# FNet mixing with a hard-swish MLP: gathers for the special piece of x, the first two weight pieces joined behind x, the last piece folded and multiplied in two parts

## The chip, the cores and the metric

The kernel runs on one core of a Trainium2 chip. The metric is the device time of one execution in microseconds (us), as the median of several runs. The core has a matrix engine (TensorE, "PE", with its weight loads "PEld"), a vector engine (VectorE, "DVE"), a scalar engine (ScalarE, "ACT"), GpSimd ("POOL") and SyncE ("SP"), which here only issues DMAs. DMAs are issued by SP, ACT and POOL; 16 DMA engines carry them all.

## The reference

The input x is (8, 3008, 256). A 2D Fourier transform is taken over the last two axes and its real part kept; an MLP with hard-swish follows.

```python
X = np.fft.fft(x, axis=1)
X = np.fft.fft(X, axis=2)
x = X.real.astype(np.float32).reshape(B * S, D)     # 24064 tokens of 256
h = x @ w_in                                        # w_in 256 x 2048
g = h * np.clip(h + 3.0, 0.0, 6.0) / 6.0
out = g @ w_out                                     # w_out 2048 x 256
```

## The kernel before

**Factoring.** 3008 is 47 x 64, so a position is a row n1 (47 of them) and a column n2 (64). Stage 1 transforms over n1, stage 2 over n2; the transform over the 256 features is folded into w_in (`fold_w_in`, L788: a product with the table C gives W1, and its last row, sent by a DMA of one column at a time, gives WN). Before stage 1 x is folded: each element is added to its partner at the mirrored position, so that only 32 of the 64 columns remain.

**Pieces of x.** A batch of x is cut into pieces of four columns. The partners of a piece lie at mirrored rows and come by an indirect DMA on POOL, a gather by a list of row numbers IX (`gather`, L172). For the first two batches one piece holds four columns m of the first half on partitions 0 to 46 and four of the second half on partitions 64 to 110. The pieces are taken in the order `ORDER` = 3, 0, 1, 2. Piece 3 is the special one: its last column, on the upper partitions, is column 0, which does not follow the others. For the first batch, `load_half` (L188) loads piece 3 by three direct DMAs on POOL's queue (two blocks of rows and the slot of column 0) and the other pieces by gathers; partners always come by gathers. For the second batch all direct rows go out on SP's queue, those of piece 3 on POOL's.

**Start.** The whole opening is written out by hand, in this order. PE runs products with zeros (`keep_awake`) so that its clock stays up. SP loads FI (which holds IX), C and the stage-1 table F. POOL issues the loads of the first two weight pieces (`load_w`), then x of the first batch, then weight pieces 2 and 3. The weights arrive as 64-bit floats (w_in and w_out are float64) and are turned into 32-bit floats: ACT takes the exponent's bytes (`exponent_a`), PE expands them (`exponent_b`), ACT makes them a power of two (`exponent_c`), DVE takes the mantissa (`mantissa`) and multiplies the two (`join`); `tail` is exponent_c and join. Pieces 0 and 1 are joined and folded (`fold_w_in`) before x's folds in DVE's and PE's queues. Then, for each piece of x, DVE folds (`fold_half`, two parts) and PE does stage 1 (`stage1_early`, L304). Pieces 3 and 1 are "full": a y with sums and differences is made. Pieces 0 and 2 leave that to PE, which multiplies four column ranges instead. The results z are copied from PSUM by ACT (for the last piece one half by DVE) and written to DRAM (zd); after T, the stage-2 table, has been loaded, `load_g_half` reads the rows of the first group back as g. Stage 2 (L434), the copies q and qn, and the first chunk's products follow. POOL's next loads wait for g (`see`, L863).

**Main loop.** A chunk is 256 positions. For each of 8 steps fc, PE multiplies q with W1 (`mlp1_products`: u, v, PSUM tiles from three buffers that stage 1 and the exponents use too), DVE and ACT apply hard-swish (`activate`: s from qn, WN and u; then a), and PE multiplies a with G, the mixed w_out. In the first chunk this is the plain product (`mlp2_first`, L597), while the other weight pieces are still being converted; after it seven products replace eight (`mlp2`, L617), for which POOL adds parts of a to c (`combine`, L587) and mixes the blocks of w_out (`mix_w_out`, L777). A table in `beside` says at which step the rest is put: loads and folds of the second batch (folds on POOL), its stage 1 (`stage1_quarters`) and stage 2. All engines run their queues in the written order.

Of the kernel before, what the change touches and what calls it, by code (L numbers as in the profile page):

```python
# [7 lines left out]
F32 = mybir.dt.float32  # L8
# [5 lines left out]
AL = mybir.AluOpType  # L14
# [44 lines left out]
def kernel(  # L59
# [77 lines left out]

    ORDER = [NM - 1] + list(range(NM - 1))
    FULL = (ORDER[0], ORDER[2])

    def x_tile(pool=xpool, tag="x"):
        return pool.tile([P, XC, D], F32, tag=tag, name="xt")
# [42 lines left out]
    def take_half(hb, m, pool=xpool, tag="x"):  # L185
        hb.x[m], hb.xr[m] = x_tile(pool, tag), x_tile(pool, tag)

    def load_half(hb, m, queue):  # L188
        if hb.b == 0 and m < NM - 1:
            gather(hb.x[m], NP * NXC + m, P, D)  # L190
        for h in range(2 if hb.b or m == NM - 1 else 0):
            c = m + h * NM
            nr = N1 + 1 if h else PB
            n = XC if c < NXC - 1 else XC - 1
            rows, o = x_pn[hb.b * N1:hb.b * N1 + nr], hb.x[m][h * PB:h * PB + nr]
            queue.dma_start(out=o[:, 0:n, :], in_=rows[:, c * XC + 1:c * XC + 1 + n, :])
            if n < XC:
                queue.dma_start(out=o[:, n:XC, :], in_=rows[:, 0:1, :])
        gather(hb.xr[m], hb.b * NM + m, PX if hb.b else P)

    def fold_half(hb, m, part, eng):
        xt, xr = hb.x[m][0:PX - 1], hb.xr[m][0:PX - 1]
# [101 lines left out]
    def stage1_early(hb, m):  # L304
        cosine, sine = slice(0, P + 1), slice(P + 1, D)
        last = m == NM - 1
        y = hb.y.pop(m) if m in FULL else hb.x[m]
        pt = [ps_h.tile([P, 2, 1], F32, tag="uv", name="pt") for h in range(2)]
        ps = [bank([P, 2, D], "ps1") for h in range(2)]
        quarters = [(i, h, 1 if last and h and i else 2) for i in range(2) for h in range(2)]  # L310
        for i, h, n in quarters:
            o = pt[h][i * PB:(i + 1) * PB]
            nc.tensor.matmul(o[:, 0:n], table(5, h), y[rows(h), 2 * i:2 * i + n, P:P + 1], start=True, stop=True,
                             skip_group_check=True)
            for k in range(2 if n < 2 else 0):
                nc.tensor.matmul(o[:, 1], table(k + 1, h), y[rows(h), XC - 1 + k, P:P + 1], start=(k == 0),
                                 stop=(k == 1), skip_group_check=True)
        if m in FULL:
            for i, h, n in quarters:
                o = ps[h][i * PB:(i + 1) * PB]  # L320
                nc.tensor.matmul(o[:, 0:n], table(0, h), y[rows(h), 2 * i:2 * i + n], start=True, stop=(n == 2),
                                 skip_group_check=True)
                for k, (j, cs) in enumerate([(XC - 1, cosine), (XC, cosine), (XC - 1, sine), (XC, sine)] if n < 2 else ()):
                    nc.tensor.matmul(o[:, 1, cs], table(k + 1, h), y[rows(h), j, cs], start=False, stop=(k % 2 == 1),
                                     skip_group_check=True)
        else:
            back = slice(D - 1, P, -1)
            for k, (t, to, fr) in enumerate([(0, cosine, cosine), (0, sine, slice(1, P)),
                                             (0, slice(1, P), back), (6, sine, back)]):
                for i, h, n in quarters:  # L330
                    nc.tensor.matmul(ps[h][i * PB:(i + 1) * PB, :, to], table(t, h), y[rows(h), 2 * i:2 * i + 2, fr],
                                     start=(k == 0), stop=(k > 1), skip_group_check=True)
# [416 lines left out]
        nc.scalar.activation(exs[j].bitcast(I32), exs[j], AF.Identity, scale=2.0 ** 23)  # L749

    def mantissa(j):
        st = raw.pop(j)
# [105 lines left out]
    def tail(j):  # L858
        exponent_c(j)
        join(j)  # L860
# [10 lines left out]
                            channel_multiplier=1)  # L871
    nc.scalar.mul(E[:, 1], E[:, 0], -1.0)
    for k, m in enumerate(ORDER):
        load_half(hb, m, nc.gpsimd)
    for j in range(2, 4):
        load_w(j)
    for j in range(2):
        exponent_a(j)
        mantissa(j)
        exponent_b(j)  # L880
        keep_awake(1)
    exponent_c(0)
    exponent_c(1)
    clear_table(1)
    for j in range(2):
        join(j)
        fold_w_in(j)
    load_t(0)
    keep_awake(1)
    for k, m in enumerate(ORDER):  # L890
        for part in range(2):
# [7 lines left out]
    for j in range(4, 10):  # L899
        load_w(j)  # L900
    take_half(halves[1], ORDER[0], cpool, "c")
    load_half(halves[1], ORDER[0], nc.gpsimd)
# [12 lines left out]
    starting[0] = False  # L915
    spare = [ps_a.tile([P, 2, WB // 2], F32, tag="acc", name="spare") for h in range(2)]

# [4 lines left out]
    def beside(p):  # L922
# [7 lines left out]
        if p == 0:  # L930
            for gr in range(1, NG):
                put(gr + 1, load_t, gr)
            put(1, load_g_half, halves[0], 1)
            put(5, spread_half, halves[0], 1)
            put(NF - 1, close_w)
            for i, t in enumerate((3, 5, 7, 8)):
                put(t, mix_w_out, i)
            for gr in range(2, NSG):
                put(8 * gr - 10, load_g_half, halves[0], gr)
                put(8 * gr - 5, stage2_half, halves[0], gr)  # L940
                put(8 * gr - 4, spread_half, halves[0], gr)

            hb = halves[1]
            for k, m in enumerate(ORDER):
                if k > 0:
                    put((5, 8, 11)[k - 1], take_half, hb, m)
                    put((5, 8, 11)[k - 1], load_half, hb, m, nc.sync)
                for part in range(2):
                    put((4, 6, 11, 14)[k] + part, fold_half, hb, m, part, nc.gpsimd)
                put((8, 10, 15, 18)[k], stage1_quarters, hb, m, at=behind)  # L950
            for gr in range(NSG):
                put(8 * gr + 23, load_g_half, hb, gr)
                put(8 * gr + 27 - (gr == 0), stage2_half, hb, gr)
                put(8 * gr + 28 - (gr == 0), spread_half, hb, gr)
# [222 lines left out]
```

## Time and profile before

| | us |
|---|---|
| median of 3 runs | 1941.01 (1939.63 to 1941.74) |
| profiled execution | 1940.75 |
| its span in the trace | 1939.0 |
| PE busy | 1920.7 (99%) |
| DVE busy | 1426.0 (74%) |
| POOL busy | 1440.7 (74%) |
| ACT busy | 681.5 (35%) |
| mean granted PE clock | 0.998 |

Times in the trace count from the span's start. A group line names the source line, engine, operation and tiles, then busy time and the idle time before it with what ended it. The chain of waits follows the work that ended last back from the end; each piece has its start and length. A matmul in 32-bit floats shows as two passes. The main events of the start in the trace:

| event | us |
|---|---|
| DVE's first fold of x (L210) | 12.07 |
| PE's first stage-1 product (L313) | 15.91 |
| PE's last stage-1 pass ends | 23.40 |
| SP issues the read of g | 27.61 |
| PE's first stage-2 product (L434) | 30.43 |
| PE's first product with G (L597) | 38.37 |

### The profile page before, as it was taken

The numbers are of one execution on the slowest core, as the hardware profiler recorded it, in microseconds if no ns is written. First come the engines' busy times: TensorE is split into PE (matmuls) and PEld (weight loads), VectorE is DVE, ScalarE is ACT, GpSimd is POOL, SyncE is SP. The second block draws the span as 40 slices with busy tenths as digits, with TensorE's granted clock in tenths as the row PEclk, the third lists the DMA queues.
The fourth block names the chain that finished last, engine by engine and source line by source line (L and its number), as shares of the span: only waits on it lengthen the run. The fifth ranks groups of instructions, "written<-read, shape, count | busy, mean of one in ns | idle before, by whom it ended". The sixth has DMA issues, their size and how long they took to land.

```text
span 1939.0 us, 28126 instructions
## 1 busy us (share of the span) xinstructions
PE 1920.7 (99%) x9322; PEld 1652.9 (85%) x9322; DVE 1426.0 (74%) x2756; ACT 681.5 (35%) x1165; POOL 1440.7 (74%) x1647
## 2 busy tenths in 40 slices
PE   9999999999999999999999999999999999999997
PEld 5578888888988888888898888888899888888887
DVE  6867776767777777777787777777778777777777
ACT  6533333333333333333333333333333333333332
POOL 4397888886678877787678877878666667666664
PEclk9999999999999999999999999999999999999999
DMA  8522222311112222121111221122110101101000
GB/s 256 143 69 53 52 71 71 80 44 34 36 34 55 67 60 55 44 52 33 34 36 48 53 55 44 51 52 50 35 28 20 28 17 28 33 12 28 20 19 20
DMA packets 154472, 98.08 MB, mean 51 GB/s; under 512 B 121987, under 2 KB 136078, under 8 KB 154326
## 3 DMA queue, kind: packets, MB, share of 16 engines
q1 hardware_dynamic: 142898, 59.25, 12.6%
q0 software_dynamic: 10720, 36.81, 6.8%
q8 instruction: 73, 1.20, 0.3%
q14 instruction: 73, 0.60, 0.1%
q10 hardware_dynamic: 708, 0.23, 0.1%
HBM read 58.92 MB, written 37.32 MB: 50 GB/s over the span
## 4 chain that ended last, share of the span: by engine, by line
PE 93%; DVE 2%; POOL 1%; DMA 1%; ACT 1%; issue 1%; SPq 0%; ACTq 0%; DVEq 0%; POOLq 0%
PE acc L617 56%; PE v L524 16%; PE u L524 16%; PE ps L473 2%; PE ps L274 1%; PE acc L597 1%; POOL c L587 1%; DVE a L573 1%; DVE s L533 0%; PE ps L434 0%; ACT t L570 0%; PE spare L798 0%; DVE o L678 0%; DMA st<-in_moe_w_in_dram 0%; DMA WN<-W 0%
## 5 line engine op out<-in xcount | busy, mean ns | idle before, releaser
L587 POOL TENSOR_TENSOR c<-a 128x512 f32<-128x512 f32 (+1 forms) x375 | 469.3, 1251 | 352.4 <-PE acc L617 286.7
L617 PE MATMUL acc<-c,G 128*128 128x256 f32 (+1 forms) x3008 | 697.6, 375 | 1.2 <-POOL c L587 1.1
L570 ACT ACTIVATE t<-u,half 128x512 f32<-128x512 f32 (+1 forms) x384 | 260.7, 679 | 1145.0 <-DVE u L543 1065.5
L617 PEld LDWEIGHTS acc<-c,G 128*128 128x128 f32 x3008 | 565.0, 190 | 73.4 <-POOL c L587 2.4
L533 DVE SCALAR_TENSOR_TENSOR s<-qn,WN,u 128x256 f32<-128x256 f32 (+1 forms) x768 | 330.4, 471 | 345.0 <-PE u L524 337.8
L617 PE MATMUL acc<-a,G 128*128 128x256 f32 (+1 forms) x2256 | 541.6, 375 | 0.0
L617 PEld LDWEIGHTS acc<-a,G 128*128 128x128 f32 x2256 | 421.0, 189 | 73.6 <-issue 20.1
L524 PE MATMUL v<-q,W 127*128 127x256 f32 (+1 forms) x1536 | 389.6, 375 | 3.1 <-DVE a L573 3.1
L524 PE MATMUL u<-q,W 128*128 128x256 f32 (+1 forms) x1536 | 388.0, 375 | 0.2 <-ACT q L437 0.2
L573 DVE SCALAR_TENSOR_TENSOR a<-t,u 128x512 f32<-128x512 f32 (+2 forms) x448 | 263.9, 601 | 101.5 <-ACT t L570 98.3
L524 PEld LDWEIGHTS v<-q,W 127*128 127x128 f32 x1536 | 288.0, 190 | 44.0 <-DVE a L573 3.4
L524 PEld LDWEIGHTS u<-q,W 128*128 128x128 f32 x1536 | 285.8, 190 | 36.9 <-issue 1.9
L587 POOL TENSOR_TENSOR c<-a,c 128x256 f32<-128x256 f32 (+1 forms) x375 | 269.0, 717 | 29.4
L587 POOL TENSOR_TENSOR c<-c,a 128x256 f32<-128x256 f32 (+1 forms) x375 | 269.0, 717 | 29.4
L543 DVE TENSOR_TENSOR u<-s,v 128x512 f32<-128x512 f32 x352 | 245.1, 696 | 37.7 <-DVE s L533 1.4
L573 DVE SCALAR_TENSOR_TENSOR a<-t,v 128x512 f32<-128x512 f32 (+1 forms) x480 | 263.5, 565 | 1.1 <-ACT t L570 0.6
L570 ACT ACTIVATE t<-v,half 128x512 f32<-128x512 f32 (+1 forms) x384 | 260.8, 679 | 1.6 <-issue 1.0
L545 DVE TENSOR_TENSOR v<-v,s 128x512 f32<-128x512 f32 x352 | 243.9, 693 | 0.0
L587 POOL TENSOR_TENSOR r<-w,e 128x256 f32<-128x256 f32 (+1 forms) x92 | 88.8, 987 | 3.6
L627 ACT ACTIVATE e<-acc 128x512 f32<-128x512 f32 (+2 forms) x184 | 83.4, 544 | 0.0
L678 DVE STREAM_TRANSPOSE o<-r 128x256 f32<-128x256 f32 (+1 forms) x192 | 72.5, 415 | 0.2
L587 POOL TENSOR_TENSOR w<-w,e 128x512 f32<-128x512 f32 (+1 forms) x46 | 57.6, 1252 | 3.6
(128 smaller groups left out, 776.8 us busy)
## 6 DMA issues: line engine op xcount, KB each, us to landing
out_dram<-o SPq DMA_DIRECT2D x747, 32.0 KB
g<-zd SPq DMA_DIRECT2D x42, 256.0 KB
zd<-z SPq DMA_DIRECT2D x48, 192.0 KB
xt<-in_x_dram POOLq DMA_DIRECT2D x23, 256.0 KB
st<-in_moe_w_in_dram POOLq DMA_DIRECT2D x8, 512.0 KB
st<-in_moe_w_out_dram POOLq DMA_DIRECT2D x8, 512.0 KB
qn<-qd SPq DMA_DIRECT2D x16, 256.0 KB
xt<-in_x_dram POOLq DMA_DIRECT2D x17, 192.0 KB
```

What stands on the lines that cost most here:

```text
L274: nc.tensor.matmul(ps[b][h * PB:(h + 1) * PB, 0:n], F[rows(b), 0:PB], y[rows(b), 2 * h:2 * h + n], start=True, stop=not last, skip_group_c ...
L473: nc.tensor.matmul(ps[:, blk, u * P:n].rearrange("p (b k) -> p b k", b=2), g[:, kk, blk * (P + 1):blk * (P + 1) + P], T[:, :, gr, blk, kk, ...
L524: nc.tensor.matmul(ps[:, i, 0:nq], W1[r, blk, f * P:(f + 1) * P], q[r, blk, of:of + nq], start=True, stop=True)
L533: nc.vector.scalar_tensor_tensor(s[:, i, 0:nq], qn[:, of:of + nq], WN[:, f:f + 1], u[:, i, 0:nq], op0=AL.mult, op1=AL.add)
L543: nc.vector.tensor_tensor(u[:], s[:], v[:], op=AL.add)
L545: nc.vector.tensor_tensor(v[:], v[:], s[:], op=AL.subtract)
L570: nc.scalar.activation(t, h, AF.Relu, bias=half[:], scale=scale)
L573: nc.vector.scalar_tensor_tensor(dst, t, 1.0, h, op0=AL.min, op1=AL.mult)
L587: (eng or nc.gpsimd).tensor_tensor(out, in0, in1, op=AL.add)
L617: nc.tensor.matmul(ch.acc[i // 2][:, i % 2, 0:ch.n], G[:, i, fc, :], mv, start=(fc == 0 and i % 2 == 0), stop=(fc == NF - 1), skip_group_c ...
L627: nc.scalar.mul(ch.e[:, k:i + 1, 0:ch.n], ch.acc[i // 2][:, 0:i + 1 - k, 0:ch.n], 1.0 / WS)
L678: nc.vector.transpose(o[:, 0:n // DH, h], ch.r[:, m, h, 0:n].rearrange("p (j i) -> p j i", i=DH))
```

## The change

Five edits go together.

1. The special piece of x is gathered like the others, for both batches, and the second batch's other pieces too; all are issued by POOL. The gathered piece has a wrong last column on the upper partitions. For the first batch SP loads the right one early, into a tile of its own, and ACT copies it in; for the second SP loads it into place at step 1 (`load_zero`). The kernel's tables already hold the row numbers.
2. The load of T moves from behind the first two weight folds to a place in SP's queue that now has no WN ahead of it.
3. Ahead of x only the exponents (`exponent_a`) and mantissas of weight pieces 0 and 1 remain. Their `exponent_b`, `exponent_c`, `join` and `fold_w_in` go behind stage 1 of x, mixed with pieces 2 and 3. The join of piece 3 goes behind stage 2 and the copy of qn.
4. The last piece in `ORDER` (m = 2) is folded by columns 0 and 2 first, then 1 and 3 (`fold_columns`, six operations for three), and stage 1 multiplies in the same two parts (32 products of 129 or 127 columns for 16 of 258 or 254, and eight of one column for four of two).
5. Awake products: 11 at the start for 6, and none between the first weight pieces.

On PE the queue then reads: awake 11, stage 1 of the four pieces, exponents 0 and 1, awake 2, weight folds 0 and 1, exponent 2, awake 1, exponent 3, stage 2.

```diff
+    SPLIT = ORDER[NM - 1:]
...
-    def load_half(hb, m, queue):
-        if hb.b == 0 and m < NM - 1:
-            gather(hb.x[m], NP * NXC + m, P, D)
-        for h in range(2 if hb.b or m == NM - 1 else 0):
...
-            queue.dma_start(out=o[:, 0:n, :], in_=rows[:, c * XC + 1:c * XC + 1 + n, :])
-            if n < XC:
-                queue.dma_start(out=o[:, n:XC, :], in_=rows[:, 0:1, :])
-        gather(hb.xr[m], hb.b * NM + m, PX if hb.b else P)
+    def load_half(hb, m):
+        start = hb.b * N1 * N2 * D
+        gather(hb.x[m], NP * NXC + m, P, start + D)
+        gather(hb.xr[m], m, P, start)
+
+    def load_zero(o, hb, queue):
+        queue.dma_start(out=o, in_=x_pn[hb.b * N1:(hb.b + 1) * N1, 0, :])
+
+    def zero_slot(hb):
+        return hb.x[NM - 1][PB:PB + N1, XC - 1, :]
+
+    def fold_columns(hb, m, j, eng):
+        a, r = hb.x[m][0:PX - 1, j::2, :], hb.xr[m][0:PX - 1, XC - 1 - j::-2, :]
+        for p, q in ((slice(0, P + 1, P), slice(0, P + 1, P)), (slice(1, P), slice(D - 1, P, -1)),
+                     (slice(D - 1, P, -1), slice(1, P))):
+            eng.tensor_tensor(a[:, :, p], a[:, :, p], r[:, :, q], op=AL.add)
...
+            for j in range(2) if m in SPLIT else (slice(0, 2),):
+                cols = [slice(2 * i + j, 2 * i + j + 1) if m in SPLIT else slice(2 * i, 2 * i + 2) for i in range(2)]
+                js = slice(j, j + 1) if m in SPLIT else j
+                for i, h, n in quarters if m in SPLIT else ():
+                    nc.tensor.matmul(pt[h][i * PB:(i + 1) * PB, js], table(5, h), y[rows(h), cols[i], P:P + 1],
+                                     start=True, stop=True, skip_group_check=True)
+                for k, (t, to, fr) in enumerate([(0, cosine, cosine), (0, sine, slice(1, P)),
+                                                 (0, slice(1, P), back), (6, sine, back)]):
+                    for i, h, n in quarters:
+                        nc.tensor.matmul(ps[h][i * PB:(i + 1) * PB, js, to], table(t, h), y[rows(h), cols[i], fr],
+                                         start=(k == 0), stop=(k > 1), skip_group_check=True)
...
-    keep_awake(6)
+    keep_awake(11)
     hb = halves[0]
     nc.sync.dma_start(out=FI[:], in_=c_stage1[:, 7 * PB:])
+    first_slot = qpool.tile([P, 2 * TB], F32, tag="qn", name="first_slot")
+    load_zero(first_slot[PB:PB + N1, 0:D], hb, nc.sync)
...
     for j in range(2):
         exponent_a(j)
         mantissa(j)
-        exponent_b(j)
-        keep_awake(1)
-    exponent_c(0)
-    exponent_c(1)
+    nc.scalar.copy(zero_slot(hb), first_slot[PB:PB + N1, 0:D])
     clear_table(1)
-    for j in range(2):
-        join(j)
-        fold_w_in(j)
     load_t(0)
-    keep_awake(1)
...
+    mantissa(2)
+    for j in range(2):
+        exponent_b(j)
+        exponent_c(j)
+        join(j)
     keep_awake(2)
-    for j in range(2, 4):
-        exponent_a(j)
-        mantissa(j)
-        exponent_b(j)
-        keep_awake(4 - j)
-    for j in range(2, 4):
-        tail(j)
+    exponent_a(2)
+    fold_w_in(0)
+    exponent_a(3)
+    fold_w_in(1)
+    mantissa(3)
+    exponent_b(2)
+    keep_awake(1)
+    exponent_b(3)
+    tail(2)

     stage2_half(hb, 0)
     spread_by_pe(hb, bank([P, TB], "ps3")[:])
+    tail(3)
...
             hb = halves[1]
+            put(1, load_zero, zero_slot(hb), hb, nc.sync)
             for k, m in enumerate(ORDER):
                 if k > 0:
                     put((5, 8, 11)[k - 1], take_half, hb, m)
-                    put((5, 8, 11)[k - 1], load_half, hb, m, nc.sync)
+                    put((5, 8, 11)[k - 1], load_half, hb, m)
```

More of the change, by code (lines that the diff above doesn't have):

```diff
@@ L186, in take_half @@
         hb.x[m], hb.xr[m] = x_tile(pool, tag), x_tile(pool, tag)
-    def load_half(hb, m, queue):
-        if hb.b == 0 and m < NM - 1:
-            gather(hb.x[m], NP * NXC + m, P, D)
-        for h in range(2 if hb.b or m == NM - 1 else 0):
[L192 to L195, printed above, removed]
-            queue.dma_start(out=o[:, 0:n, :], in_=rows[:, c * XC + 1:c * XC + 1 + n, :])
-            if n < XC:
-                queue.dma_start(out=o[:, n:XC, :], in_=rows[:, 0:1, :])
-        gather(hb.xr[m], hb.b * NM + m, PX if hb.b else P)
+    def load_half(hb, m):
[11 more added lines that the diff above has]
+            eng.tensor_tensor(a[:, :, p], a[:, :, p], r[:, :, q], op=AL.add)
     def fold_half(hb, m, part, eng):
@@ L310, in stage1_early @@
         quarters = [(i, h, 1 if last and h and i else 2) for i in range(2) for h in range(2)]
-        for i, h, n in quarters:
+        for i, h, n in quarters if m not in SPLIT else ():
             o = pt[h][i * PB:(i + 1) * PB]
@@ L327, in stage1_early @@
             back = slice(D - 1, P, -1)
[L328 to L332, printed above, removed]
+            for j in range(2) if m in SPLIT else (slice(0, 2),):
[9 more added lines that the diff above has]
+                                         start=(k == 0), stop=(k > 1), skip_group_check=True)
         k = ORDER.index(m)
@@ L751, in mantissa @@
     def mantissa(j):
-        st = raw.pop(j)
+        st = raw[j]
         hi = st[:].rearrange("p (n two) -> p n two", two=2)[:, :, 1]
@@ L873 @@
     for k, m in enumerate(ORDER):
-        load_half(hb, m, nc.gpsimd)
+        load_half(hb, m)
     for j in range(2, 4):
@@ L879 @@
         mantissa(j)
-        exponent_b(j)
-        keep_awake(1)
-    exponent_c(0)
-    exponent_c(1)
+    nc.scalar.copy(zero_slot(hb), first_slot[PB:PB + N1, 0:D])
     clear_table(1)
-    for j in range(2):
-        join(j)
-        fold_w_in(j)
     load_t(0)
-    keep_awake(1)
     for k, m in enumerate(ORDER):
-        for part in range(2):
+        if m in SPLIT:
+            for j in range(2):
+                fold_columns(hb, m, j, nc.vector)
+        for part in range(2) if m not in SPLIT else ():
             fold_half(hb, m, part, nc.vector)
@@ L901 @@
     take_half(halves[1], ORDER[0], cpool, "c")
-    load_half(halves[1], ORDER[0], nc.gpsimd)
-    keep_awake(2)
-    for j in range(2, 4):
-        exponent_a(j)
-        mantissa(j)
-        exponent_b(j)
-        keep_awake(4 - j)
-    for j in range(2, 4):
-        tail(j)
+    load_half(halves[1], ORDER[0])
+    mantissa(2)
+    for j in range(2):
+        exponent_b(j)
+        exponent_c(j)
+        join(j)
+    keep_awake(2)
+    exponent_a(2)
[7 more added lines that the diff above has]
+    tail(2)
     stage2_half(hb, 0)
     spread_by_pe(hb, bank([P, TB], "ps3")[:])
+    tail(3)
     starting[0] = False
```

## The prediction

> **What bounds the kernel now.** I read the page's busy table first: PE is busy 1920.7 of 1939.0 us, so only PE's few holes and the work ahead of its steady stream can be won. The list of PE's waits up to 300 us names the holes:
>
> ```profile
> PE v L524 <- DVE a L573: 2.3, 1, 2.3
> PE acc L617 <- POOL c L587: 1.1, 1, 1.1
> ```
>
> Two waits, each once. Nothing after 115 us is touched by this change (PE is 50.00 of 50.00 in most later windows), so the sum ends there. The chain of waits says what made the first hole:
>
> ```profile
> 48.32 5.17 DMA WN<-W
> ...
> 53.51 0.49 DVE s L533
> ...
> 56.29 1.49 PE v L524 x4
> 57.77 4.77 PE acc L597 x8
> ```
>
> A 0.5 KB column of WN took 5.17 us after its copy; DVE's s waited, v waited for the PSUM that s's step frees. And v and acc, normally 0.86 us for 4 passes and 3.44 for 8, took 1.49 and 4.77. The windows tell why:
>
> ```profile
> 45.00:50.00 5.00, 5.00 (x20) 3.44 (x20) 4.79 (x10) 4.39 (x8) 1.01 (x2) 1.00 1.03 248
> 50.00:55.00 5.00, 4.04 (x15) 2.10 (x13) 2.83 (x7) 2.29 (x5) 1.24 (x2) 1.00 0.91 262
> 55.00:60.00 5.00, 3.71 (x7) 2.07 (x8) 4.75 (x9) 3.47 (x6) 1.46 (x2) 0.69 0.80 276
> ```
>
> The last three columns are granted clock, DMA share and GB/s. The DMA engines were full when WN was issued; the clock fell after the hole (0.5 from 57.2 to 60.7 in the clock records). The second hole is POOL's:
>
> ```profile
> 94.91 1.27 POOL L210 TENSOR_TENSOR xt<-xt 111x508 f32<-111x508 f32 x1 [15.12 <-DMA xt<-in_x_dram]
> ```
>
> POOL stood 15.12 us for rows of x that SP issued only at 89.34, and came late with c. Before all that stands the start, whose chain is DVE's folds, then PE's stage 1:
>
> ```profile
> 21.56 1.83 PE ps L331 x32
> ...
> 30.43 1.14 PE ps L434 x8
> ...
> 38.53 1.72 PE acc L597 x4
> ```
>
> Stage 1 ends at 23.40; the first product with G (L597) starts at 38.4.
>
> **Arrival of x.** By the trace's packet records POOL's transfers complete at 7.81 (second weight piece), 10.01 (special piece's direct rows), then every 1.28 us (gathers): 11.49 for its partners, 16.60 for the partners of the third piece, 19.18 for those of the last. The change makes 2.20 us of direct rows one gather (-0.92) and puts 256 KB of T (moved up from 17.85) and 47 KB of the slot ahead of them: 303 KB at the windows' 400 GB/s is +0.76. Net -0.16.
>
> The slot can cost more. A 48-row zd write left 16 completion packets in the records, a 24-row zq write 12, as if the rows were divided evenly over the engines. 47 divides by no number up to 16, so all 47 packets of 1 KB may lie on one engine: at 0.055 us each (C's packets) 2.6 us, of which some 0.6 falls into that engine's idle time. Every later gather also needs that engine, so x may come 0 to 2.0 us later; gathers' completions spread by 0.8 us over the engines, so I take 1.1. The Trainium skill, "DMA: Bandwidth & Descriptors", section "Why a DMA increments its semaphore by 16 and not by 1", says that a DMA issued from SP runs on the largest count up to 16 that divides its rows. By that rule it is one engine and the sum nears its upper end; without it, the lower. The 12 completions agree.
>
> **Folds and stage 1.** The joins leave DVE's queue ahead of the folds, and the first fold, held until 12.07 by them, can start when its partners are there: 11.4 with x on time. The folds take 7.74 us (12.07 to 19.81) up to the last piece's, so that starts at 19.2 at best. With x 1.1 late, the third fold starts at 17.5 and the last at 20.15. Its three operations (1.36 us) become six; one of 254 elements starts the next after 0.34 (between 0.2 at 127 and 0.5 at 381), so 1.5 in all, but PE may begin after 0.45. PE runs twice the passes at half the columns. The rows: 0.057 a pass of 258 columns, 0.036 a pass of 1 or 2. 80 passes take 2.1 (half the time each) to 2.9 (0.036 each), against 2.12; I take 2.6. The third piece's products start 0.2 after the last fold and take 1.23, so PE has its turn at 20.6 with x on time and 21.6 with x late. **Stage 1 ends at 24.2**, between 22.7 (even spread, short passes) and 25.4, where it was 23.40: +0.8. The slot's copy on ACT (0.23 for 112x2, 0.59 for 112x512) lies beside the first fold and is free; without that cover it would cost about 0.4.
>
> PE's 11 awake products hide in the wait: 22 passes, five at 0.855 and 17 at 0.43, end near 13.3. Then PE is idle to about 15.5. Idle of 2.4 us from 53.9 halved the clock, so here it may fall too, costing stage 1 up to 1.4 us if x is on time, nearly nothing if it is late, as PE then waits anyway. The Trainium skill, "TensorE: Matmul & The Clock Gate", Part 1, has the clock fall after an idle window of about 3.4 us and warns of gaps over that. By that this gap is safe and the hole at 53.9 would have been; the trace differs at 2.4 us, and it decides.
>
> **From stage 1's end to the first product with G.** Before, 15.0 us, of which 7.0 to L434 were waits for zd, g, and awake products. The zd writes were held up by semaphores of the WN columns and T queued ahead of them on SP; the last was issued at 25.3, 1.2 us after its z. Now it goes at once: last zd landed 3.3 after stage 1's end (2.46 from ACT's issue), g 2.73 later, **6.1**. But the moved work is now on PE: two exponent pairs (0.87), two awake (1.72), join at 2.8 after the end on DVE, two fold_w_in (3.46, ready at 6.5), a pair, awake, a pair (1.7): L434 starts at **8.2**. So PE, not g, ends last, and 2.1 us of g's gain is given away. Then ps2 and ps3 (1.35) to 9.55, ACT's copies of q and qn to 10.1, exponent_c(3) behind them to 10.7, join 3 (0.75) to 11.5, and in DVE's queue behind that s of chunk step 0 (u was done at 10.9). u of step 1 needs join 3's PSUM: 11.6 to 12.45, three awake products (2.58) to 15.05, v to **15.9**, where the product starts: +0.9. WN's needed columns are issued at 7.6; with a free DMA they land at 9.3 (1.35 to the first packet, as g), with a full one at 12.8, when s's second half would wait 0.7. The new weight loads' packets start about 8.2 (2.1 after g), so I take nothing, and 0.7 for the range.
>
> Start in all: 0.8 + 0.9 = **+1.7**, from +0.2 to +3.6.
>
> **The WN hole.** POOL's loads of pieces 4 to 9 follow g, at 30.3 (23.4 to 24.2 plus 6.1), as before; they land by 42.4. Next came 896 KB for the second batch's special piece in four transfers, 42.38 to 47.98. Two gathers of 512 KB now: 1.28 to 1.6 us each, done by 45.6, and two weight pieces (1.45 each) by 48.5. WN is issued at 48.3 + 1.7 = 50.0, and the next weight piece (gated by ACT at 47.8) brings packets only after 51. So WN lands in about 1.7 us, and s (50.97 on the old clock, behind DVE's join) no longer waits: a's u half ends 3.17 us after s, v starts at 54.2 instead of 56.29, 0.3 after u. acc ends at 58.5 instead of 62.55: **-4.05**, of which 2.1 is the hole and 1.95 the lost clock. Next late are s (57.0 + 1.7) and PE's weight folds, with DVE's joins done 2 us ahead. The clock part is chance in each execution: 2.1 alone is the lower bound.
>
> **The POOL hole.** The second pieces are gathers on POOL: three more at 1.1 us, issued at 78.8 and landed by 84, ten us before POOL's 94.9. The second G mix must wait for PE's products of steps 4 and 5 (88.3), the folds end near 93.5, then c of step 8 follows its a (98.3), a mix of 3.2, two gathers of 2.2, and c of step 9 starts at 106.6 instead of 110.01. PE asks for it at 110.3. **-1.07**; bounds 0 and -1.07. SP loses six issues and gains one 47-row load, needed by POOL 10 us later: nothing. If POOL's cover were gone, each gather would cost PE 1.1.
>
> **Sum:** 1940.75 + 1.7 - 4.05 - 1.07 = **1937.3**. That is the profiled execution's own time (span 1939.0); the median shown is 1941.01, 0.26 above. 0.2%, about what a measurement of this kernel can tell from no change, is 3.9 us: faster means below 1937.1.
>
> **Rivals.**
> - *x on time* (slot spread over the engines): start +0.2 to +1.0, time 1935.8 to 1936.6. For it: a small load of 47 KB is done before the gathers need much. Against: the completion counts.
> - *The slot on one engine, its 2.0 us in full*: stage 1 ends at 25.4, start +2.9, time 1938.5. For it stand the completion counts, against it the spread of 0.8 that may hide a part; it is the forecast's upper part, with 0.15 of the chance. (This is the rule of the Trainium skill, "DMA: Bandwidth & Descriptors", named above.)
> - *WN waits as before*, the other side: q0 is still full at 50 us (gathers at the 160 GB/s of the direct rows, 42.4 to 48.0, instead of 400). Then the hole and lost clock stay, the start's cost is unpaid: 1940.75 + 1.7 - 1.07 = 1941.4; with the late slot and WN's first column late (+3.6) and POOL's hole kept, 1944.4. It decides if POOL's last load ahead of WN ends after 50.
> - *The loads don't free POOL* (gathers wait for a buffer): 1938.4.
> - *The clock falls in the start's new gap* with x on time: 1.4 more, 1937.6.
>
> **Chances.** Forecast with its upper part 0.45 (0.30 and 0.15; 0.15 of it faster), x on time 0.28 (0.26 faster), WN as before 0.16 (half of it slower), the last two 0.11 (0.02 slower, 0.04 faster). That makes 0.45 faster, 0.45 same, 0.10 slower. The range takes x on time below and WN as before above: 1935.4 to 1941.5.
>
> **What would show it.** Right: stage 1's last pass at 23 to 25.4, L434 about 8.2 after it with g landed earlier, no wait of s on WN near 52, granted clock 1.00 from 50 to 60, no wait of L617 for POOL c near 111, first L597 at 39 to 41. Wrong: completions of gathers later than 21, WN still above 3 us at 50, POOL's wait for xt near 84 to 95, or a new hole of PE behind the joins.

## The result: slower, and what the profile after shows

The changed kernel takes **1948.0 us** (median of 7 runs, 1946.85 to 1950.4), the kernel before 1940.6 in the same runs: ratio 1.0039, interval [1.0028, 1.0051]. The forecast was 1937.3, the range ended at 1941.5: wrong in sign. The profiled execution is the slowest of the seven, 1950.4 with a span of 1948.7, so its sums lie 2.4 above the median. From the second group of stage-1 products of the second batch on (L371 at 125.39, L360 at 115.40 before) it runs 10.0 later than before, and at the end 9.7: the whole loss has been made by then.

PE's waits up to 300 us (total, times, longest), which before named the WN hole (PE waits for a, because s waits for WN) and the POOL hole (PE waits for c):

```profile
PE v L535 <- DVE a L584: 4.1, 3, 2.8
PE pt L318 <- DVE y L228: 3.3, 1, 3.3
```

The wait for POOL's c is gone, as forecast. The wait for a is no longer one of 2.3 but three, the longest 2.8; and there is a new one of 3.3 ahead of the first stage-1 product. What lies behind the latter is in the chain of waits up to 58 us (start, length, what):

```profile
5.02 9.04 DMA xt<-in_x_dram,IX
...
26.17 1.79 PE ps L342 x26
27.97 0.12 PE pt L337 x5
28.09 2.36 PE ps L342 x32
...
38.96 7.51 DMA WN<-W
46.50 0.49 DVE s L544
```

From the issue of the first piece's second gather to its last landing pass 9.04, and DVE's first fold starts at 14.16 (12.07 before). Stage 1 ends at 28.09 + 2.36 = 30.45 (23.40 before). A column of WN then takes 7.51, more than the 5.17 that the change was to shorten, and the first product with G starts at 50.72 (38.37 before). The windows (busy time of PE, PEld, DVE, ACT and POOL with counts, then granted clock, DMA share, GB/s) show why stage 1 is slow:

```profile
15.00:20.00 5.00, 2.59 (x24) 2.11 (x25) 4.75 (x16) 1.47 (x4) 0.37 (x1) 0.67 1.03 409
20.00:25.00 5.00, 5.00 (x59) 4.49 (x61) 3.42 (x10) 1.99 (x6) 0.00 (x0) 0.50 0.59 188
25.00:30.00 5.00, 5.00 (x87) 4.61 (x80) 0.00 (x0) 1.80 (x7) 0.00 (x0) 0.50 0.33 53
30.00:35.00 5.00, 5.00 (x13) 2.23 (x12) 4.03 (x7) 2.97 (x5) 0.00 (x0) 0.62 0.14 26
...
50.00:55.00 5.00, 5.00 (x12) 2.17 (x12) 2.36 (x5) 2.44 (x5) 1.50 (x2) 0.66 0.47 146
```

PE's timeline shows the gap:

```profile
17.10 0.44 PE L318 MATMUL pt<-y,F 47*64 47x2 f32 x8 [3.34 <-DVE y L228]
```

PE idles from 13.77 to 17.10, the clock goes to 0.5 at 16.74 and **stays there until 33.81**, five windows of 3.41 us in the clock records, with PE busy 5.00 of 5.00 from 20 to 30. It falls once more from 50.88 to 54.29, behind the new wait of v (2.76, 46.99 to 49.75). POOL's fold of the second batch, which before stood 15.12 for rows of x, now stands 4.49 and is in time:

```profile
96.80 1.26 POOL L215 TENSOR_TENSOR xt<-xt 111x508 f32<-111x508 f32 x1 [4.49 <-DMA xt<-in_x_dram,IX]
```

**Theory:** the clock's fall in the new gap is the loss; it lasts 17 us, not one window. **Rivals:** the joins behind x (a longer way from stage 1 to the first product), or the late x by itself.

### The profile page after: what moved, and what is told of

It reads as the page before. It is cut to its first block, busy times and chain, and to the rows that moved or that the text cites. A ratio compares the mean times of both kernels' runs of the same rounds, so it can differ in the third digit from the quotient of the medians.

```text
span 1948.7 us, 28199 instructions
## 1 busy us (share of the span) xinstructions
PE 1928.2 (99%) x9362; PEld 1660.2 (85%) x9362; DVE 1425.6 (73%) x2759; ACT 680.8 (35%) x1166; POOL 1440.8 (74%) x1646
## 4 chain that ended last, share of the span: by engine, by line
PE 94%; DVE 3%; DMA 1%; ACT 1%; issue 0%; POOL 0%; DVEq 0%; SPq 0%; ACTq 0%; POOLq 0%
PE acc L628 56%; PE v L535 16%; PE u L535 16%; PE ps L484 2%; PE ps L279 1%; PE acc L608 1%; DVE a L584 1%; DMA WN<-W 1%; DVE s L544 1%; ACT t L581 1%; DMA xt<-in_x_dram,IX 0%; PE ps L342 0%; DVE o L689 0%; DVE u L565 0%; PE ps L445 0%
## 5 line engine op out<-in xcount | busy, mean ns | idle before, releaser
L535 PE MATMUL v<-q,W 127*128 127x256 f32 (+1 forms) x1536 | 389.4, 375 | 4.9 <-DVE a L584 4.9
L535 PE MATMUL u<-q,W 128*128 128x256 f32 (+1 forms) x1536 | 388.0, 375 | 0.2 <-ACT q L448 0.2
L535 PEld LDWEIGHTS v<-q,W 127*128 127x128 f32 x1536 | 287.9, 190 | 46.3 <-DVE a L584 6.4
L535 PEld LDWEIGHTS u<-q,W 128*128 128x128 f32 x1536 | 285.8, 190 | 36.9 <-issue 1.9
```

Source lines behind the costliest of these rows:

```text
L535: nc.tensor.matmul(ps[:, i, 0:nq], W1[r, blk, f * P:(f + 1) * P], q[r, blk, of:of + nq], start=True, stop=True)
```

## The experiments

Every kernel has its ratio to the kernel before, run beside it (medians 1939.7 to 1940.9). The table gives events of the profiled executions; "hole" is PE's wait for a ahead of the L535 product that WN sets, its start between 53 and 69.

| kernel | median (range), us | ratio to before, interval | first fold | stage 1 ends | first L608 | hole |
|---|---|---|---|---|---|---|
| after | 1948.0 (1946.85 to 1950.4) | 1.0039 [1.0028, 1.0051] | 14.16 | 30.45 | 50.72 | 1.10 |
| e1: slot 48 rows | 1944.94 (1942.93 to 1948.29) | 1.0024 [1.0015, 1.0033] | 12.23 | 27.8 | 44.97 | 1.09 |
| e2: awake 15 | 1939.24 (1938.83 to 1944.83) | 0.9996 [0.9987, 1.0005] | 14.20 | 25.3 | 41.41 | 0.91 |
| e3: both, awake 13 | 1937.69 (1937.48 to 1938.31) | 0.9985 [0.9976, 0.9994] | 12.39 | 23.5 | 39.60 | 1.06 |
| e4: joins ahead | 1937.63 (1937.16 to 1938.06) | 0.9986 [0.9977, 0.9995] | 14.41 | 25.4 | 39.50 | 1.12 |
| e5: joins ahead, 48 rows | 1936.18 (1935.75 to 1936.41) | 0.9978 [0.9968, 0.9987] | 12.51 | 23.5 | 38.36 | 1.03 |
| e6: before + second batch | 1936.96 (1936.39 to 1937.84) | 0.9981 [0.9972, 0.9990] | 12.44 | 23.6 | 38.88 | 1.09 |
| e7: loads later | 1945.71 (1944.78 to 1946.13) | 1.0025 [1.0015, 1.0034] | 13.93 | 30.2 | 47.59 | 1.12 |
| e8: e3, last piece whole | 1937.82 (1937.52 to 1938.36) | 0.9987 [0.9978, 0.9996] | 12.44 | 23.7 | 39.78 | 1.11 |
| e9: e5, special piece later | 1937.15 (1936.39 to 1937.63) | 0.9982 [0.9973, 0.9991] | 12.72 | 23.7 | 37.91 | 0.86 |
| e10: awake inside | 1947.92 (1947.01 to 1948.05) | 1.0034 [1.0020, 1.0049] | 13.75 | 33.9 | 50.01 | 1.12 |
| e11: e5, T late | 1936.01 (1935.55 to 1936.93) | 0.9973 [0.9964, 0.9983] | 11.96 | 22.9 | 38.38 | 0.98 |
| e12: e5, columns two and two | 1936.28 (1936.01 to 1936.96) | 0.9982 [0.9973, 0.9991] | 12.58 | 23.7 | 38.11 | 1.03 |

**e1: the slot as 48 rows** instead of 47, for both batches (one row more is loaded and copied, and not used).

```diff
-in_=x_pn[hb.b * N1:(hb.b + 1) * N1, 0, :]
+in_=x_pn[hb.b * N1:(hb.b + 1) * N1 + 1, 0, :]
```

> Changed kernel, but the slot of column 0 is loaded as 48 rows instead of 47 (one row more, which nothing reads), so that its packets can be divided over 16 engines. Theory (47 rows lie on one DMA engine, which holds back every gather; the late x opens a gap of PE, the clock falls, and stage 1 runs at half clock): completions of POOL's transfers no longer lag by 1 to 2 us on one engine, DVE's first fold starts at 12.0 to 12.5 instead of 14.16, PE's gap shrinks from 3.3 to 1.5 us, the clock stays at 1.00, stage 1 ends at 23.5 to 24 instead of 30.45; time 1942 (1941 to 1943). Rival (T and the gathers themselves are what delays x): the first fold stays at 14 or later, time 1948. Rival (the joins behind x are the cost): first fold earlier, but time 1946 or more.

x comes 1.93 earlier (first fold 12.23), and the 16 parts of a POOL transfer end together: in the packet records of the changed kernel 15 of the 16 completions of POOL's first transfer lie by 5.50 and the next one is at 7.85; here all 16 lie by 5.79. The slot's own load, issued at 1.28, shows a single late mark on its semaphore in the changed kernel, at 5.91; here it shows sixteen, from 2.82 to 3.12. So the 47 rows did lie on one engine. But PE's gap of 1.40, with another of 0.40 behind it, was not short enough; that part of the expectation fell, and with it the time (1942 expected). The clock went down at 16.77 and came back at 30.42:

```profile
15.00:20.00 5.00, 4.43 (x58) 3.98 (x62) 4.80 (x16) 1.62 (x6) 0.59 (x1) 0.68 1.03 408
20.00:25.00 5.00, 5.00 (x70) 4.30 (x66) 1.54 (x7) 2.38 (x6) 0.00 (x0) 0.50 0.62 194
```

3.1 of the 7.4 us are the slot's, by way of one window less at half clock and by x itself; most of the loss is still there. (The profiled execution, 1942.93, is the fastest of the 11.)

**e2: four more awake products**, the slot as in the changed kernel.

```diff
-    keep_awake(11)
+    keep_awake(15)
```

> Changed kernel with 15 awake products at the start instead of 11, so that PE has work until about 17.2, when the first y is there. x stays late. Theory (the gap of 3.3 us drops the clock, and stage 1's small products don't bring it back): clock 1.00 through stage 1, which ends at 25.5 to 26 instead of 30.45; time 1943.5 (1942.5 to 1944.5). Rival (stage 1's small products alone let the clock fall): the clock falls one window later, stage 1 ends after 28, time 1947 to 1948.

The gap shrinks to 0.92, the clock is 1.00 all through the start, and 8.8 us are gone: 1939.24.

```profile
15.00:20.00 5.00, 3.68 (x50) 2.40 (x52) 4.75 (x16) 2.42 (x5) 0.21 (x1) 1.00 1.03 407
20.00:25.00 5.00, 4.32 (x120) 3.40 (x116) 3.49 (x10) 2.95 (x11) 0.00 (x0) 1.00 0.72 208
```

Nothing else was touched, x is as late as in the changed kernel. Late x alone is therefore not the loss. The expected 1943.5 was 4.3 too high: stage 1 ended as expected (25.3), but the expectation counted its gain alone, and with the clock up the wait for WN's first column and the second fall are gone as well. One of its 11 runs took 1944.83, with a granted clock of 0.995 where the others have 0.998 or 0.999; so in that run the clock most likely fell, and a gap of 0.92 is not safe each time.

**e3: both edits**, `keep_awake(13)` and 48 rows.

> Both: 48 rows for the slot and 13 awake products. Theory: no lag, no gap, clock 1.00, stage 1 ends near 23.3; what is left over before is the longer way from there to the first product (0.9 or, with WN's column late, up to 5) and the gains of the two holes; time 1940 to 1942. Rival (joins behind x cost more than they free): 1943 or more. If the holes' gains come in full as predicted, 1937.

The gap is 0.23, and stage 1's windows have the clock that they had before. First the kernel before, then this one:

```profile
15.00:20.00 5.00, 4.63 (x71) 2.89 (x69) 4.92 (x13) 2.75 (x9) 0.90 (x2) 1.00 1.03 397
20.00:25.00 5.00, 4.94 (x60) 2.57 (x61) 2.71 (x6) 2.53 (x10) 0.00 (x0) 1.00 0.68 187
```

```profile
15.00:20.00 5.00, 4.02 (x69) 3.23 (x68) 4.82 (x14) 2.04 (x7) 0.77 (x2) 1.00 1.02 406
20.00:25.00 5.00, 4.66 (x102) 3.35 (x103) 3.04 (x11) 2.75 (x9) 0.00 (x0) 1.00 0.74 212
```

1937.69, 7.25 less than e1, which differs by two awake products alone. From 20 to 25 PE makes 102 passes in 4.66 us busy, where e1 made 70 in 5.00. The clock is the cause of the loss. Against e2 the slot is worth 1.55 once the clock stays up.

**e4: the third edit undone, and the fifth with it.** Joins and weight folds of pieces 0 and 1 ahead of x again, with the awake products between them and six at the start; what follows stage 1 has its old order again. The slot of 47 rows and the early T stay.

```diff
-    keep_awake(11)
+    keep_awake(6)
...
         exponent_a(j)
         mantissa(j)
+        exponent_b(j)
+        keep_awake(1)
+    exponent_c(0)
+    exponent_c(1)
...
+    for j in range(2):
+        join(j)
+        fold_w_in(j)
```

> Changed kernel with the third edit undone: exponents, joins and folds of weight pieces 0 and 1 ahead of x again, six awake products at the start, the others as before; slot still 47 rows, T still early. Theory: x is as late (first fold 14.2), but PE has products up to 16, so the clock holds and stage 1 ends at 25.5 to 26; the first product with G follows 15 us later at 41, not 20 us; time 1943 (1942 to 1944.5). Rival (only the joins' place is the cost, not x's lateness): 1940.6 or less. Rival (their place does not matter): 1946 to 1948.

1937.63: with the joins ahead of x, PE has work of its own and its longest wait up to 30 us, but for the first 1.7, is 0.48. The clock stays up with x as late as in the changed kernel (first fold 14.41). The third edit made the gap by taking PE's work away from there. The expected 1943 was missed by 5.4, for the reason named at e2. The time is the one of the rival by which only the joins' place costs and late x costs nothing (1940.6 or less); e5 answers that part.

**e5: the third edit undone and 48 rows.**

> The changed kernel with the joins and weight folds of pieces 0 and 1 ahead of x again (as e4) and the slot loaded as 48 rows (as e1). Theory: in e4 the end of stage 1 (25.4) is set by late x alone, and stage 2 follows it by about 6.1 as it waits for g; so x on time brings the first fold to 12.1 to 12.5 (where the joins ahead of it hold it), stage 1's end to 23.5, the first stage-2 product to about 29.7 (31.6 in e4) and the time to 1635.8 + 300 = 1935.8. Rival: the joins and weight folds ahead of x cost as much as late x did, and the start stays as in e4: 1937.6. With the clock at full speed throughout in both.

1936.18, as the theory had it within 0.4 (its 1935.8 is e4 less some 1.9 of stage 1). Beside e3 (1937.69) only the place of the joins and the awake products differ: the joins behind x cost 1.5 even with the clock up. Beside e4 the slot is worth 1.45, about as between e2 and e3 (1.55); so late x does cost something, but little beside the clock.

**e6: the kernel before with the second batch's half of the first edit alone.**

```diff
     def load_half(hb, m, queue):
+        if hb.b:
+            start = hb.b * N1 * N2 * D
+            gather(hb.x[m], NP * NXC + m, P, start + D)
+            gather(hb.xr[m], m, P, start)
+            return
...
+            put(1, load_zero, zero_slot(hb), hb, nc.sync)
```

> The kernel before with the second half of the first edit alone: x of the second batch by gathers on POOL, its slot by one load at step 1; the start is that of the kernel before. Theory: the first hole (PE's wait for a near 54, 2.3 us before) shrinks to about 1.1 as in e3 and e4, no loss of clock follows it (1.95 us in the profiled execution of before), and PE's wait for POOL c near 110 (1.1 us) is gone: with e4 less its later start (1.1 us at the first product with G), about 1936.5. Rival: the hole and the fall of the clock stay, as the gathers keep the DMA engines full as long as the direct rows did, and only POOL's hole goes: 1939.4.

1936.96, 3.3 below the kernel before beside it (ratio 0.9981 [0.9972, 0.9990]). The hole falls from 2.25 to 1.09, no loss of clock follows, PE's wait for c is gone; of its waits for a this is left:

```profile
PE v L535 <- DVE a L584: 1.3, 2, 1.1
```

This one half gives most of what the best kernel here has; the rest of the change (first batch by gathers, T, the parts of the last piece) adds 0.8 in e5.

**e7: the loads of weight pieces 4 to 9 and the second batch's special piece** wait for the second weight fold's copy instead of g.

```diff
-    see(hb.g[0][:, 0, 0:1])
...
     fold_w_in(1)
+    see(W1[:, 0, in_column(0, 1):in_column(0, 1) + 1])
+    for j in range(4, 10):
+        load_w(j)
```

> The changed kernel, but POOL's loads of weight pieces 4 to 9 and of the second batch's special piece wait for the second weight fold's copy into W1 and no longer for g. Theory: WN's first columns came late (7.51 us) because those loads had filled the DMA engines ahead of them. Then WN lands about 2 us after its copies, DVE's s of the first step no longer waits 3.05 for it, PE's hole of 2.76 near 47 to 50 and the second fall of the clock (51.2 to 54.6) are gone, and the first product with G follows stage 1's end by about 16 instead of 20.3: some 4 to 5 us less, 1943.5, or up to 1.2 us more where the later loads hold up WN's next columns. Rival: WN is late for SP's own queue or ACT's copies at the half clock: 1948, with the hole still there.

The first product with G comes at 47.59 instead of 50.72 and s waits for no WN; the second fall of the clock is gone:

```profile
45.00:50.00 5.00, 5.00 (x17) 2.52 (x16) 3.89 (x7) 3.99 (x7) 2.03 (x3) 1.00 1.02 386
50.00:55.00 5.00, 5.00 (x21) 3.47 (x20) 4.19 (x8) 3.90 (x7) 0.46 (x1) 1.00 1.00 391
```

Where the changed kernel has PE busy 2.24 of 5.00 from 45 to 50, this has 5.00. So the 7.51 us of WN were the loads ahead of it. The median is 2.3 lower, the profiled execution 4.7 (1945.73 against 1950.4); the expectation of 4 to 5 holds for the latter alone, and its 1943.5 was missed by 2.2. In the changed kernel's other runs, which have no profile, the granted clock speaks for a second fall in two of the seven: it is 0.993 in the two of 1950.1 and 1950.4, and 0.994 or 0.995 in the five of 1946.9 to 1948.2 and in all of e7.

**e8: e3 with the fourth edit undone** (`SPLIT = ()`).

> e3 (the changed kernel with the slot as 48 rows and 13 awake products) with the fourth edit undone: the last piece folded and multiplied as one. By the prediction's sizes the split lets PE begin the last piece 0.9 us earlier and costs 0.5 us more in products: undone, stage 1 ends 0.4 later, and the time is 1938.1. Rival: the split costs more than it saves (half-width products at 0.036 a pass), undone 1937.3 or less.

1937.82 against 1937.69, ranges over one another, stage 1's end 0.2 later. The two parts of the last piece give and cost nothing that can be told.

**e9: what is left of the WN hole.** e5 with the special piece of the second batch issued at step 2.

```diff
-    load_half(halves[1], ORDER[0])
...
-            put(1, load_zero, zero_slot(hb), hb, nc.sync)
+            put(2, load_half, hb, ORDER[0])
+            put(2, load_zero, zero_slot(hb), hb, nc.sync)
```

> e5, but the two gathers of the second batch's special piece are issued at step 2 of the first chunk and no longer behind weight piece 9; its slot comes right behind them. Theory: what is left of the WN hole (1.03 us at 55.07 in e5, s waits 0.95 for WN) is made by these two transfers ahead of WN in the DMA engines; WN then lands in about 2 us, the hole falls to 0.1 or less, 1935.2. Rival: the weight pieces behind them take their place in the queue, and the hole stays at 1.0: 1936.2; and if the gathers come late for POOL's folds near 61, POOL's c is late again, 1937.

Missed: the hole went from 1.03 to 0.86 only, and the time rose by 1.0. A new hole of 1.40 opened, which ends at 72.51: POOL's folds now start 3.5 later (64.64 against 61.14), beside other steps of DVE's weight conversion, and those steps take longer (below, last section). The rival's time, 1937, came, but not by its way: PE has no wait for c.

**e10: where the clock comes back.** Six products with zeros right behind the first piece's stage 1.

```diff
         stage1_early(hb, m)
+        if k == 0:
+            keep_awake(6)
```

> The changed kernel with six products with zeros (12 passes of 512 columns) right behind the first piece's stage 1. A measurement of what lifts the clock: in the changed kernel it stayed at 0.5 from 17.06 to 34.13, though PE was busy nearly all of that time with stage 1's products of 64 columns of weights on 47 rows. If only full-size products lift it, it goes to 1.00 at 23.9 or 27.3, a window of 3.41 us behind the first full-size ones, and stage 1's products behind them take half their time again. If it rises by the time since it fell, it stays at 0.5 until 34.13, and the time is 5 to 10 us longer than the changed kernel's 1948.

The clock fell at 15.37 and was back at 25.61, 10.2 us and not 17.1 later. PE's timeline and the windows:

```profile
20.61 7.88 PE L826 MATMUL awake<-Z,ones 128*128 128x512 f32 x12
...
28.56 1.93 PE L342 MATMUL ps<-xt,F 47*64 47x258 f32 x32
```

```profile
20.00:25.00 5.00, 5.00 (x9) 2.13 (x8) 3.00 (x10) 0.65 (x2) 0.00 (x0) 0.50 0.57 180
25.00:30.00 5.00, 5.00 (x44) 2.50 (x46) 0.00 (x0) 0.22 (x2) 0.00 (x0) 0.94 0.00 0
```

The full-size products begin at 20.61. Counted from the fall in windows of 3.41, they take 1.59 of the one that ends at 22.20, behind which the clock stays down, and all of the next, which ends at 25.61, where it rises. The 32 passes of the second piece behind them take 1.93; at the half clock of the changed kernel they took over 3.25 (0.21, then 3.04 for 26, in its chain). The time is the changed kernel's own (1947.92): the products cost 7.9 and stage 1 ends 3.5 later, but the first product with G comes 0.7 earlier, as WN's first column is in time, and no second fall follows. So it is the kind of work, not the time since the fall, that lifts the clock. e1 agrees: there the clock rose at 30.42, behind a window with 2.73 us of full-size products (from stage 1's end at 27.76), 13.65 us after its fall.

**e11: e5 with T behind the weight folds again**, as in the kernel before.

> e5 with the second edit undone: T is loaded behind the first two weight folds, as in the kernel before. By the prediction's size T ahead of x costs x 0.64 us (256 KB at 400 GB/s), but in e5 the first fold (12.51) waits for the joins and not for x, so nothing comes back: 1936.2, and up to 0.8 more if the zd writes and g wait behind T and WN on SP's queue as they did before. Rival: the folds behind the first one do wait for x in e5, and T late gives 0.6 back: 1935.6.

The first fold comes 0.55 earlier (11.96) and stage 1 ends 0.6 earlier, the price of T that I had; that the first fold wouldn't move was wrong. But stage 2 starts at 30.44 (30.39 in e5), held 0.91 by g instead of 0.32, so nothing comes back. 1936.01 and 1936.18 can't be told apart. It is the fastest here: 0.9973 [0.9964, 0.9983].

**e12: e5 with WN's columns sent two and two** instead of one and three.

```diff
-        wait = [] if k else fs[1:]
+        wait = []
```

> e5 with another order of WN's columns: each weight fold sends both of its columns at once (two and two), where the first fold sent one and the second three. In e5 the three were issued one behind the other, 0.57 each, from 48.32 to 50.1, and their packets all lie behind 51.41, 1.3 after the last issue; with the second batch's transfers out of the way (e9) it was the same, 1.1 after the last issue. Theory: the rest of the hole (1.03 at 55.07) is these issues: with two in the row the packets come 0.57 earlier, s waits 0.4 and the hole is 0.46: 1935.6. Rival: the DMA engines are full of weight pieces at that time (0.8 to 0.9 in e9 from 49 on) and set the landing, however few columns are issued: hole 1.0, 1936.2.

The hole is 1.03 again, as the rival had it. With one column less in the row, WN still takes as long, by the chains of e5 and of this kernel:

```profile
48.32 3.95 DMA WN<-W
```

```profile
48.06 3.96 DMA WN<-W
52.01 0.02 issue
52.04 0.49 DVE s L544
```

Neither the transfers ahead of WN (e9, which took 0.17 off) nor the number of columns (e12) explains what is left. The DMA view of e9 from 44 to 56 (40 slices of 0.3 us, busy tenths and GB/s) shows what may be:

```profile
DMA  5200000001100000859897696885589988954899
GB/s 219 109 14 0 0 27 0 0 0 1 1 0 0 0 0 0 177 164 314 314 410 287 98 124 151 154 188 147 195 277 318 274 322 295 226 168 191 314 410 400
```

The engines are nearly empty until 48.8; then the weight piece that POOL issued at 47.40 fills them. The columns are issued behind it, from 47.87, and their packets come from 50.45, with that load's first completion. In e5 and e12 too the columns' packets begin within 0.01 of it (51.09; 50.75 and 50.76). That this load is what holds WN is read from the order of events; it was not tried.

## Why the prediction was wrong

**The step that failed** is the price of the clock: "Idle of 2.4 us from 53.9 halved the clock, so here it may fall too, costing stage 1 up to 1.4 us if x is on time, nearly nothing if it is late, as PE then waits anyway." That it may fall was right; the price was not, nor the claim that late x hides it. 1.4 us is what a fall of less than one window of 3.41 us can cost, like the one in the trace before; how long this one would last the prediction does not ask. Measured: 17.07 us at 0.5 with x late, 13.65 in e1, and 8.8 us (changed kernel to e2) or 7.25 (e1 to e3) of time. Stage 1's products at half clock are PE's longest work by far, so it no longer waits for x, and they do not lift the clock again: the fall feeds itself until the first full-size products behind stage 1 (30.45). In the profiled executions (1950.4 and 1939.15 in e2) it is worth 5.1 up to stage 1's end (30.45 against 25.33), 1.2 more up to stage 2 (39.83 against 33.55), 3.0 more up to the first product with G (50.72 against 41.41), most of which is the wait for WN (2.76), and an estimated 1.7 in the second fall (half of 3.41): 11.0 of 11.25. The rival that held this case had the right mechanism, and a price of 1.4.

The Trainium skill, "TensorE: Matmul & The Clock Gate", Part 1, lets the clock fall after an idle window of about 3.4 us and rise after about 3.4 us of sustained work. The first was already off in the trace before (2.25 of idle), and in e1 the clock fell behind 1.79 of idle (1.40 and 0.40) in a window whose rest held full-size and small products. The second differs too: from 20.5 to 30 PE was busy all the time and the clock did not rise. (The clock's times in the prediction and in the expectation for e10 are 0.32 late against the windows: 0.69 from 55 to 60 asks for a fall at 56.9, not 57.2. Nothing in the argument hangs on it.)

**The second miss** is WN's first column: "The new weight loads' packets start about 8.2 (2.1 after g), so I take nothing, and 0.7 for the range." The loads' packets start 8.3 after stage 1's end (38.75), as forecast; but the columns, forecast for 7.6, are issued 8.5 after it (38.96), as PE's products ahead of the weight folds run at half clock. So they come behind the loads' first packets, not ahead of them: POOL issues six loads of 512 KB from 37.31 on, and 4.7 of them have been started when the columns have landed. s waits 3.05, PE 2.76, and the clock falls again. e7 gives back 3.1 at the first product. With the clock up the columns are issued 7.4 after stage 1's end (e2, e3) and are in time.

**The third** is a size: the WN hole was to vanish (-4.05), and 0.9 to 1.1 of its 2.25 stays in every kernel. The loss of clock behind it does vanish in all of them. What was wrong: "the next weight piece (gated by ACT at 47.8) brings packets only after 51"; in e9 they come at 48.9, in e5 at 49.3.

**What held.** One engine for the 47 rows: x came some 1.8 late (14.16 against 12.2 to 12.5 with 48 rows), near the 2.0 of the upper end, which the 12 completions of a 24-row write and the rule cited from the Trainium skill pointed to; I had taken 1.1. With the clock up stage 1 ends at 25.3 (forecast: 25.4 with the slot in full) and, with x on time, at 23.5 (the forecast's 20.6 and 2.1 to 2.9 give 22.7 to 23.5). The way there differs: the first fold, forecast for 11.4 with x on time, starts at 12.2 to 12.4 with 48 rows (e1, e3). So x came 0.8 to 1.0 later than the forecast had it even without the slot's delay; why is open. L445 follows stage 1's end by 8.2 in e3, as forecast, the first product by 16.1 (15.9). The POOL hole is gone (-1.07). With two sizes mended the sum gives 1937.3 + 0.9 for the slot in full + 1.0 for the hole that stays = 1939.2, and e2, where the clock stays up, has 1939.24. That it agrees so closely is luck in part: e2's first product with G is 3.0 later than before (41.41 against 38.37), where the mended sum has 2.6. The moved joins cost 1.24 at the first product (39.60 in e3, 38.36 in e5), forecast 0.9.

The rival that the joins behind x are the loss holds for 1.5 of it at most; late x alone falls by e2, and is worth 1.45 to 1.55 once the clock stays up. T (e11) and the two parts of the last piece (e8) are worth less than 0.2 each, which can't be told from nothing; the gathers of the first batch were not tried alone.

## What to carry to other kernels

When PE's work is moved away from a place where it waits, price the gap by the work that follows it: small products behind a gap can run at half clock until full-size ones come, so count every pass up to there twice, and keep PE busy with full-size products up to the first small one. A change with several edits is worth taking apart: here one half of one edit gives 3.3 us and another edit loses more than all. And a load whose rows all lie on one DMA engine delays every transfer that uses all 16; one row more can mend it.

## What the runs showed of the hardware

- Small products (64 columns of weights on 47 rows) hold the clock up (e3, 1.00 from 15 to 25) but don't lift it (changed kernel, 13.0 us busy at 0.5); full-size ones (128 by 128, 512 columns) do. It rose behind windows of 3.41 us with 3.41 (changed kernel, e10) and 2.73 us (e1) of them, not behind one with 1.59 (e10). Whether the size of the weights or the number of columns counts was not tried.
- It fell behind windows with 2.25 (before) and 1.79 us (e1) of idle; 1.31 in e2's window from 14.79 to 18.20 did not let it fall in the profiled run.
- A load of 47 KB in 47 rows put one of the 16 parts of the next queue's transfer 2.35 us behind the others (completions at 5.50 and 7.85); with 48 rows the last two were 0.03 apart.
- A column of 0.5 KB took 7.51 among six loads of 512 KB (changed kernel); with those loads later, s did not wait for it (e7).
- DVE's conversions lengthen beside POOL's tensor work. In e9, beside POOL's folds and mixes, and then in e5, while POOL has nothing to do from 65.05 to 69.30:

```profile
64.81 1.22 DVE L768 TENSOR_SCALAR top<-st 128x512 int32<-128x512 int32 x1
66.07 1.23 DVE L769 SCALAR_TENSOR_TENSOR top<-st,top 128x512 f32<-128x512 uint32 x1
```

```profile
65.98 0.42 DVE L768 TENSOR_SCALAR top<-st 128x512 int32<-128x512 int32 x1
66.43 0.69 DVE L769 SCALAR_TENSOR_TENSOR top<-st,top 128x512 f32<-128x512 uint32 x1
```

The same two instructions take 2.45 and 1.11. The Trainium skill, "SBUF — State Buffer", section "SBUF: two separate sides", has GpSimd and VectorE share one pair of ports, which one of them holds for a whole instruction, where the VectorE operation runs in a two-port mode or has two inputs in SBUF. These rows agree; e9's chain runs through them up to the v at 72.51, so they are the likely reason that two gathers put late cost 1.0 us there.
